# Moving type casts from GpSimd to VectorE and ScalarE, with a new first-load queue and a new order, in a fused attention and SoLU kernel on one Trainium2 core

## The chip, the core and the metric

The kernel runs on one core of a Trainium2 chip. A core has five engines with an instruction queue each: TensorE (PE in the profile, with its weight loads shown apart as PEld), VectorE (DVE), ScalarE (ACT), GpSimd (POOL) and SyncE (SP), which here only issues transfers. All share an on-chip memory (SBUF); matmul results go to a smaller one (PSUM). The engines run side by side and wait for one another through semaphores; each works through its own queue strictly in order. The metric is device time in microseconds (us). The kernel before takes 179.88 us, the median of three runs (179.87 to 180.01).

## What is computed

Batch 4, 8 heads, 768 positions, head dimension 64, 8 global keys, a local window of 96, followed by a 512 to 1024 to 512 feed-forward stage with a SoLU activation and a layer norm:

```python
scores = scale * q @ k.T + bias            # bias: -slope[h] * distance (capped for global keys)
keep   = key is global or 0 <= i - j < 96
a      = softmax(where(keep, scores, -1e9))
x      = (a @ v), heads side by side       # 3072 tokens x 512
h      = x @ w_in                          # 512 -> 1024
solu   = h * softmax(h)
out    = ((solu - mean) / sqrt(var + 1e-6) * g_ln) @ w_out   # 1024 -> 512
```

## The kernel before

The 3072 tokens are cut into twelve **units** of 256 query positions, three for each batch (units 0, 3, 6 and 9 open a batch and have no block of keys to their left). A unit goes through these steps, named by short codes; a number after the code is the unit, a second one a half, a pair of heads or a block of 128 tokens.

- `q`, `k`, `v`: loads of 256 KB each, two for each tensor of a unit, as 32-bit numbers into a ring of 13 staging tiles. The letter in the step is the queue: `S` SyncE, `A` ScalarE, `P` GpSimd.
- `cq`, `ck`, `cv`: the cast of a staged tile of 128 x 1024 from 32 to 16 bits (letter: `D` VectorE, `A` ScalarE, `P` GpSimd). It also frees the staging tile. Lines 138, 140 and 142 are the three engines' casts, in the helper `cast`.
- `tq`, `tk`: eight transposes on TensorE (line 300); `eq`, `ek`: their copy from PSUM (lines 138 and 140 too).
- `S` scores (line 323), `X` exponential (ScalarE, line 332), `M` multiplication by the mask (VectorE, line 339); `gS`, `gX` the same for the global keys, whose keys `gk` (line 314) picks on GpSimd.
- `L` row sums by a matmul with ones (line 385) and with the heads' selector `hm` for the global keys (line 393), `I` their inverse (ScalarE, lines 401 and 402), `V` values, `N` normalisation (VectorE, line 430). `gv0` and `gv` prepare the global values.
- Feed-forward for each 128 tokens: `A` first matmul (line 446), `E` exponential (ScalarE, line 460), `U` product (VectorE, line 468), `Q` squares (ScalarE, line 477), `Z` five tiny operations on GpSimd for the layer norm (lines 492 to 499), `d` a transpose by DMA on SyncE's queue, `O` second matmul (line 522), `o` scaling from PSUM (lines 534 and 536), `st` store.
- Once: `mask` the 16 mask slices on ScalarE from the distances `dist` (VectorE) that come from GpSimd's `off`; `wi` and `wo` the weights' loads; `sc`, `mean`, `ce`, `cm`, `pr`, `sm` fold `g_ln` and the centring into `w_out`. `warm` is a run of matmuls on zeros.

Nothing is planned at run time. A string, `ORDER`, lists all 670 steps, and each engine's queue holds its own steps in the order of that string. What stands ahead of a step on its engine must be done first, whether the step needs it or not. Buffers limit it too: three large PSUM tiles for scores, sums, values and the first feed-forward matmul together, two small ones, and the 13 staging tiles.

In the string before, GpSimd does 23 of the 36 casts, VectorE 10 and ScalarE 3. The opening loads are spread over three queues: `k:P:2:0` and `k:P:2:1` on GpSimd's, `k:A:0:0`, `k:A:0:1`, `k:A:1:1` and `v:A:0:1` on ScalarE's, the rest on SyncE's.

Of the kernel before, what the change touches and what calls it, by code (L numbers as in the profile page):

```python
# [32 lines left out]
q:S:3:1 wi:0 ck:D:5 v:S:1:0 v:S:1:1 ck:P:4 k:P:6:0 k:S:6:1 v:S:2:0 wo:S:6 S:1:3 X:0:1 M:0:1 X:0:2
M:0:2 X:1:0 gX:1 mask:1:4 gv:0 S:1:1 k:S:8:0 X:1:1 mask:1:5 tq:2 M:0:0 X:1:3 eq:D:2 tk:3 M:1:3
ek:D:3 S:1:2 X:1:2 S:2:1 X:2:1 M:2:1 S:2:0 X:2:0 gS:2 gX:2 S:2:2 X:2:2 cq:P:4 M:1:2 M:1:1 M:1:0
S:2:3 X:2:3 M:2:0 M:2:2 tk:4 ek:A:4 cq:P:3 gk:1 wi:2 v:P:2:1 v:S:3:0 wo:S:0 ck:P:6 v:P:3:1 L:0 I:0
tq:4 eq:D:4 L:1 I:1 cq:D:5 tq:3 eq:D:3 k:S:8:1 wo:S:2 q:P:6:0 q:S:6:1 wo:S:4 warm:5:3 V:0 M:2:3
N:0 cv:D:1 S:3:0 X:3:0 S:3:2 X:3:2 tk:5 ek:D:5 gS:4 gX:4 S:3:1 X:3:1 S:4:1 X:4:1 V:1 N:1 M:3:2
q:S:7:0 q:S:7:1 v:S:4:0 v:S:4:1 M:4:1 k:S:7:0 S:3:3 X:3:3 M:3:3 S:4:0 gS:3 X:4:0 tk:6 ek:D:6 S:4:3
X:4:3 gX:3 M:4:0 S:4:2 X:4:2 M:4:3 A:0:0 E:0:0 cv:A:2 A:1:0 E:1:0 A:1:1 M:3:1 U:0:0 M:4:2 Q:0:0  # L40
Z:P:0:0 v:S:5:0 k:S:9:0 tq:5 q:S:8:0 d:S:0:0 cv:P:3 gv0:1 L:2 U:1:0 eq:D:5 E:1:1 U:1:1 M:3:0
d:S:1:0 I:2 sc:D:0 ck:P:8 k:S:10:0 d:S:1:1 A:0:1 E:0:1 v:P:6:0 U:0:1 sc:P:3 sc:A:7 sc:A:6 pr:7
sc:P:2 gS:5 V:2 N:2 gX:5 L:3 I:3 cq:D:6 sc:D:1 gv:1 L:4 I:4 S:5:0 tk:8 ek:D:8 sc:P:4 sc:A:5 A:2:0
E:2:0 U:2:0 X:5:0 tq:6 S:5:1 eq:A:6 X:5:1 mean ce:0 cm ce:1 ce:2 ce:3 ce:4 k:P:7:1 A:2:1 E:2:1
U:2:1 Q:1:1 warm:12 S:5:3 X:5:3 ck:D:7 V:3 cq:P:7 v:P:6:1 S:5:2 pr:6 cv:P:4 N:3 V:4 N:4 k:P:9:1
q:P:8:1 pr:5 sm:5 gk:2 sm:6 Q:2:1 X:5:2 cv:A:6 sm:7 k:P:10:1 M:5:0 tk:7 ek:D:7 S:6:0 S:6:2 X:6:0
M:5:3 Z:P:1:1 gv0:2 Q:0:1 X:6:2 Q:1:0 tq:7 eq:D:7 Z:P:1:0 A:4:0 E:4:0 U:4:0 A:3:0 E:3:0 U:3:0
S:7:2 gS:6 gX:6 O:0:0 o:D:0:0 M:5:2 X:7:2 M:7:2 Q:2:0 v:P:7:0 cq:P:8 q:S:10:0 q:S:10:1 v:S:5:1
q:S:9:0 d:S:0:1 O:1:0 o:D:1:0 Q:3:0 M:5:1 Z:P:3:0 S:6:3 S:6:1 X:6:3 X:6:1 M:6:1 cv:D:5 S:7:0 X:7:0
d:S:3:0 ck:P:9 O:1:1 gS:7 S:7:1 X:7:1 M:7:1 M:7:0 ck:P:10 v:P:7:1 Z:P:0:1 k:S:11:0 k:P:11:1  # L50
q:S:11:0 ck:P:11 d:S:2:0 v:S:9:0 v:S:8:0 cq:D:10 o:A:1:1 S:7:3 X:7:3 cv:P:7 Z:P:2:0 L:5 I:5 A:3:1
M:6:0 E:3:1 M:7:3 gX:7 M:6:2 Q:4:0 Z:P:4:0 U:3:1 A:4:1 O:0:1 E:4:1 tk:9 ek:A:9 o:D:0:1 st:S:0
U:4:1 M:6:3 V:5 N:5 v:S:9:1 q:S:9:1 tq:8 eq:A:8 tk:10 ek:D:10 L:7 I:7 S:8:1 X:8:1 gv:2 A:5:1 E:5:1
st:S:1 v:S:11:0 U:5:1 L:6 I:6 Q:5:1 O:2:0 o:D:2:0 V:6 S:8:3 X:8:3 N:6 gk:3 v:P:11:1 v:P:8:1 S:8:2
Q:3:1 Z:P:3:1 O:3:0 o:A:3:0 X:8:2 M:8:3 cq:D:9 tq:10 A:6:1 E:6:1 eq:D:10 gS:8 gX:8 U:6:1 d:S:2:1
V:7 N:7 S:8:0 X:8:0 Q:4:1 d:S:3:1 tk:11 ek:D:11 M:8:2 M:8:1 d:S:4:0 q:S:11:1 cv:P:9 gv0:3 cq:P:11
Z:P:2:1 tq:9 eq:A:9 A:5:0 E:5:0 U:5:0 A:6:0 E:6:0 U:6:0 gS:10 S:10:0 X:10:0 O:3:1 o:D:3:1 gX:10
Q:5:0 S:10:3 X:10:3 S:9:2 X:9:2 d:S:4:1 d:S:6:0 d:S:5:0 A:7:0 E:7:0 U:7:0 tq:11 eq:D:11 S:10:2
X:10:2 S:10:1 X:10:1 O:2:1 o:D:2:1 M:10:1 Q:6:0 M:8:0 st:S:2 v:S:10:0 st:S:3 A:7:1 Z:P:4:1 cv:P:11
cv:P:8 O:4:0 o:D:4:0 Q:7:0 Q:6:1 E:7:1 d:S:5:1 d:S:6:1 L:8 I:8 S:11:2 X:11:2 M:10:3 U:7:1 M:10:2  # L60
d:S:7:1 gS:11 gX:11 Z:P:6:1 O:4:1 M:10:0 o:D:4:1 M:11:2 Z:P:7:0 v:P:10:1 V:8 N:8 S:11:1 Z:P:5:1
X:11:1 S:11:3 X:11:3 gv:3 O:6:0 S:11:0 X:11:0 S:9:3 X:9:3 Z:P:6:0 L:10 I:10 M:9:3 M:11:1 o:D:6:0
S:9:1 X:9:1 M:9:1 M:11:0 M:9:2 cv:A:10 d:S:7:0 st:S:4 Z:P:5:0 O:5:0 A:8:0 E:8:0 U:8:0 d:S:8:0
o:A:5:0 A:8:1 M:11:3 E:8:1 U:8:1 V:10 gS:9 gX:9 O:6:1 N:10 L:11 I:11 S:9:0 X:9:0 M:9:0 A:10:0
E:10:0 O:5:1 o:A:5:1 o:D:6:1 U:10:0 V:11 L:9 I:9 V:9 N:11 A:11:0:0 A:11:0:1 st:S:6 st:S:5 Q:7:1
Q:8:1 N:9 E:11:0:0 U:11:0:0 d:S:8:1 O:7:0 A:11:1:0 A:11:1:1 o:D:7:0 Q:8:0 Z:P:7:1 Q:11:0:0
E:11:0:1 Z:P:8:0 U:11:0:1 A:9:0 O:7:1 o:D:7:1 st:S:7 Q:10:0 E:11:1:0 U:11:1:0 E:9:0 E:11:1:1
U:11:1:1 O:8:0 t:11:0:0 t:11:0:1 e:D:11:0:0 e:A:11:0:1 o:A:8:0 Z:P:8:1 A:10:1 E:10:1 Q:11:0:1
Z:P:11:0:1 U:9:0 d:S:9:0 d:S:10:0 O:8:1 Q:9:0 Z:P:9:0 Q:11:1:0 Z:P:10:0 O:11:0:0 O:11:0:1
o:A:11:0:0 U:10:1 o:A:11:0:1 Q:10:1 o:D:8:1 st:A:11:0:1 A:9:1 t:11:1:0 t:11:1:1 O:9:0 e:D:11:1:0  # L70
st:S:8 e:D:11:1:1 E:9:1 U:9:1 d:S:10:1 d:S:9:1 O:10:0 O:11:1:0 O:11:1:1 Q:11:1:1 o:A:9:0 O:10:1
Z:P:11:1:1 o:D:11:1:1 st:S:11:1:1 o:D:11:1:0 st:S:11:1:0 st:S:11:0:0 Q:9:1 o:A:10:0 Z:P:10:1
o:A:10:1 st:S:10 O:9:1 Z:P:9:1 o:A:9:1 st:S:9 warm:4:4 warm:5:2 warm:4:5 warm:5:1
"""


# [587 lines left out]
```

## Time and profile before

| what | value |
|---|---|
| time, median of three | 179.88 us |
| profiled span | 178.8 us |
| TensorE busy | 157.3 us, 88% |
| ScalarE busy | 143.8 us, 80% |
| VectorE busy | 125.0 us, 70% |
| GpSimd busy | 107.9 us, 60% |
| DMA | 34.35 MB, mean 192 GB/s |

The shares are averages over stages with different limits, so they are to be read together with the row of 40 slices, which shows the busy tenths of each engine along the span (one slice is 4.47 us). Matmuls are pipelined and their ends modelled, so a TensorE that is shown busy may still be waiting a little between matmuls. The longest waits of the whole trace, summed by line, begin like this (waiting engine and line, what it waited for, us in total, times, longest):

```profile
POOL w L497 <- ACT sq L477: 21.7, 6, 14.1
DVE un L468 <- ACT e L460: 12.7, 11, 2.8
PEld L300 <- POOL q L142: 12.6, 4, 7.4
PE qturned L300 <- POOL q L142: 11.4, 2, 7.4
```

The first is GpSimd idling in the layer norm's small operations; the last two are TensorE waiting for GpSimd's cast of `q`, 7.4 us of it before the very first transpose.

### The profile page before, as it was taken

Reading aid. Unit: us, or ns where it says so; the run is one execution under the profiler, and the core shown is the slowest. Engines: PE = TensorE matmul, PEld = TensorE weight load, DVE = VectorE, ACT = ScalarE, POOL = GpSimd, SP = SyncE. Lnnn points to the kernel's source line nnn. Section 1 sums busy time; section 2 is a strip of 40 time slices with the busy share of each in tenths; the row PEclk is TensorE's granted clock in tenths of the full one; section 3 lists DMA queues with packets and bytes.
Section 4 is the critical chain, followed back from the end, with each engine's and each line's share of the span. In section 5 each row is a group of like instructions: output and inputs, shape, how many; then the busy total and the mean of one; then the engine's idle time right before and its main releaser. Section 6 shows DMA issues by size and latency. Waiting matters only on the chain. (4 is left out here: it accounts for less than half of the span.)

```text
span 178.8 us, 4095 instructions
## 1 busy us (share of the span) xinstructions
PE 157.3 (88%) x1551; PEld 86.0 (48%) x1551; DVE 125.0 (70%) x185; ACT 143.8 (80%) x231; POOL 107.9 (60%) x214
## 2 busy tenths in 40 slices
PE   0227689889995899999999999999999999999987
PEld 0115267564562347445475564545545564544432
DVE  3660999999999579899894878389468364473310
ACT  2474999899999568999979998998893969778720
POOL 8347985721699658779847878708780006407870
PEclk9999957999999699999999999999999999999999
DMA  4999999999999972069999870339991583147553
GB/s 124 341 347 341 339 287 279 356 283 307 235 213 232 274 226 56 6 117 226 156 238 298 187 139 0 59 60 141 292 135 29 176 286 70 49 114 219 114 188 142
DMA packets 50547, 34.35 MB, mean 192 GB/s; under 512 B 41120, under 2 KB 41632, under 8 KB 50528
## 3 DMA queue, kind: packets, MB, share of 16 engines
q1 hardware_dynamic: 45648, 26.35, 61.9%
q0 software_dynamic: 2224, 6.56, 13.6%
q10 hardware_dynamic: 2656, 1.18, 2.4%
q8 instruction: 12, 0.20, 0.5%
q14 instruction: 7, 0.06, 0.1%
HBM read 23.07 MB, written 6.29 MB: 164 GB/s over the span
## 5 line engine op out<-in xcount | busy, mean ns | idle before, releaser
L446 PE MATMUL ph<-w_in,xT 128*128 128x512 f16 x192 | 44.3, 379 | 0.2
L522 PE MATMUL po<-gw,uT 128*128 128x512 f16 x192 | 44.3, 379 | 0.1
L332 ACT ACTIVATE pt<-sc 128x896 f16<-128x896 f32 (+1 forms) x48 | 39.7, 866 | 3.4 <-PE sc L323 3.2
L468 DVE SCALAR_TENSOR_TENSOR un<-e,ph 128x1024 f16<-128x1024 f16 (+1 forms) x26 | 29.4, 1134 | 14.4 <-ACT e L460 12.7
L339 DVE TENSOR_TENSOR pt<-pt,mask 128x896 f16<-128x896 f16 (+1 forms) x48 | 30.0, 659 | 7.9 <-ACT pt L332 7.9
L446 PEld LDWEIGHTS <-xT 128*128 128x128 f16 x192 | 18.2, 98 | 21.5 <-issue 1.0
L522 PEld LDWEIGHTS <-uT 128*128 128x128 f16 x192 | 18.0, 98 | 21.4 <-DMA uT<-un 0.4
L460 ACT ACTIVATE e<-ph 128x1024 f16<-128x1024 f32 (+1 forms) x26 | 24.7, 953 | 2.5 <-DVE un L468 1.2
L477 ACT ACTIVATE sq<-un 128x1024 f16<-128x1024 f16 (+1 forms) x26 | 25.8, 992 | 0.5 <-DVE un L468 0.2
L300 PE MATMUL qturned<-ident,q 128*128 128x128 f16 x96 | 8.6, 242 | 14.6 <-POOL q L142 11.4
L497 POOL TENSOR_SCALAR w<-s,w 128x1 f32<-128x1 f32 x22 | 7.3, 331 | 23.4 <-ACT sq L477 21.7
L323 PE MATMUL sc<-qT,kT 64*128 64x128 f16 (+2 forms) x256 | 15.7, 244 | 1.2 <-DVE xT L430 0.8
L401 ACT ACTIVATE rlb<-lb 128x1024 f32<-128x1024 f32 x12 | 12.3, 1027 | 5.0 <-PE lb L393 5.0
L430 DVE TENSOR_TENSOR xT<-pa,rlb 128x1024 f16<-128x1024 f32 x12 | 14.5, 1218 | 2.1 <-ACT rlb L402 1.7
L499 POOL TENSOR_TENSOR rs<-w,neghalf 128x1 f32<-128x1 f32 x24 | 14.0, 582 | 2.0
L300 PEld LDWEIGHTS <-q 128*128 128x128 f16 x96 | 6.8, 108 | 16.7 <-POOL q L142 12.4
L140 DVE COPY kT<-kturned 128x1024 f16<-128x1024 f16 x9 | 10.8, 1214 | 5.6 <-PE kturned L300 5.6
L534 DVE TENSOR_SCALAR osb<-po,rs 128x512 f32<-128x512 f32 (+1 forms) x15 | 10.6, 712 | 5.4 <-POOL rs L499 2.7
L492 POOL TENSOR_SCALAR w<-s 128x1 f32<-128x1 f32 x22 | 8.6, 393 | 9.1 <-ACT e L460 7.1
L402 ACT ACTIVATE rlb<-rlb 128x1024 f32<-128x1024 f32 x12 | 12.7, 1057 | 0.4
L142 POOL CAST k<-k 128x1024 f16<-128x1024 f32 x8 | 9.2, 1154 | 6.0 <-PE kturned L300 4.9
L495 POOL TENSOR_SCALAR w<-mean,w 128x1 f32<-128x1 f32 x24 | 11.0, 458 | 2.4
(87 smaller groups left out, 243.8 us busy)
## 6 DMA issues: line engine op xcount, KB each, us to landing
...
```

What stands on the lines that cost most here:

```text
L300: nc.tensor.transpose(out=t[:, r], in_=src[:, r].rearrange("p m d -> p (m d)"), identity=held["ident"])
L323: nc.tensor.matmul(out=sc[:, m, o : o + e - a], lhsT=held["kT", u - s + j // 2][r, g, ts(j % 2, P)], rhs=qT[r, g, a:e], start=True, stop=True,
L332: nc.scalar.activation(out=pt[:, :, 0:w], in_=held.pop(("sc", u, g))[:, :, 0:w], func=AF.Exp, scale=inv_sqrt_d)
L339: nc.vector.tensor_tensor(out=pt[:, :, 0:w], in0=pt[:, :, 0:w], in1=held["mask"][:, g, :, o : o + w], op=ALU.mult)
L402: nc.scalar.activation(out=rlb, in_=rlb, func=AF.Exp, scale=-1.0)
L430: nc.vector.tensor_tensor(out=xT.rearrange("p g (r i) -> p g r i", r=2), in0=held.pop(("pa", u)).rearrange("p g (i r) -> p g r i", r=2), i ...
L446: nc.tensor.matmul(out=held["ph", t][:, ts(fh, 512)], lhsT=held["xT", t[0]][:, j, ts(t[1], P)], rhs=held["w_in"][:, j, ts(fh, 512)], start ...
L460: nc.scalar.activation(out=held["e", t][:, f], in_=held["ph", t][:, f], func=AF.Exp, accum_out=s0)
L468: nc.vector.scalar_tensor_tensor(out=held["un", t][:, f], in0=held["e", t][:, f], scalar=1.0, in1=held["ph", t][:, f], op0=ALU.mult, op1=A ...
L477: nc.scalar.activation(out=sq[:, f], in_=held["un", t][:, f], func=AF.Square, accum_out=s2)
L499: eng.tensor_tensor(out=rs, in0=w3, in1=held["neghalf"], op=ALU.pow)
L522: nc.tensor.matmul(out=held["po", t], lhsT=held["uT", t][:, c, :], rhs=held["gw"][:, c, :], start=(c == 0), stop=(c == NFC - 1),)
```

## The change

Four things are done at once.

1. From the fourth unit on, the casts go to VectorE and ScalarE. GpSimd keeps the first three units' (`ck`, `cq` of 0 and 1, `ck` of 2, `cv` of 0, 1 and 2): 8 casts for 23. VectorE has 24 for 10, ScalarE 4 for 3.
2. The first units' loads leave GpSimd's queue and ScalarE's. All `q`, `k` and `v` of units 0 and 1 are issued by SyncE, in the order of need. GpSimd's queue issues 20 loads in all for 23.
3. In `L` the global keys' sums come first and open the accumulation; the local blocks follow.
4. The whole order is new: the two `off` and `dist` steps open GpSimd's and VectorE's queues, unit 0's two transposes are first on TensorE, unit 4's scores come ahead of unit 3's, and so on to the end. The copies `eq`/`ek` stay 17 on VectorE and 7 on ScalarE, though of other units.

The aim is to relieve GpSimd and let the first units begin sooner. The mask's tile is now allocated in `mask`, since a mask is no longer preceded by `cap`. The diff, with the order cut to its beginning:

```diff
 ORDER = """
-zero g:A id gb k:P:2:0 cap off:1 dist:1 fill k:P:2:1 off:0 dist:0 k:A:0:0 k:A:0:1 ck:D:0 q:S:0:0
-q:S:0:1 cq:P:0 tq:0 eq:D:0 hm q:S:1:0 k:S:3:0 q:S:1:1 q:S:2:0 k:S:1:0 k:S:3:1 v:S:0:0 q:S:2:1
-k:S:5:0 mask:1:7 k:A:1:1 mask:0:7 mask:0:0 mask:0:4 selV v:A:0:1 tk:0 cq:P:1 mask:0:1 mask:1:2
-mask:1:1 tq:1 mask:0:2 mask:0:5 ek:A:0 S:0:0 S:0:3 mask:0:6 ck:D:2 tk:2 ek:D:2 k:P:5:1 ck:P:1 tk:1
-ek:D:1 ck:P:3 S:0:1 gk:0 gS:0 eq:A:1 mask:1:3 gS:1 X:0:3 M:0:3 mask:0:3 mask:1:6 mask:1:0 S:0:2
...
+q:S:0:0 k:S:1:0 k:S:0:0 off:1 off:0 zero dist:1 mask:1:0 mask:1:4 id cap dist:0 mask:0:2 mask:0:1
+mask:0:5 mask:0:4 k:S:0:1 ck:P:0 tk:0 ek:D:0 q:S:0:1 cq:P:0 tq:0 k:S:1:1 ck:P:1 q:S:1:0 gb tk:1
+ek:D:1 q:S:1:1 q:S:2:0 q:S:2:1 cq:D:2 mask:1:5 mask:0:0 mask:1:1 mask:0:6 mask:1:6 mask:1:3 eq:A:0
+mask:0:3 S:0:0 gk:0 S:0:2 gS:0 X:0:0 X:0:2 S:0:3 k:S:3:0 S:0:1 X:0:1 cq:P:1 gX:0 fill hm X:0:3
+k:S:2:0 k:S:2:1 ck:P:2 mask:1:7 mask:1:2 mask:0:7 tq:1 eq:D:1 tq:2 S:1:2 X:1:2 S:1:0 X:1:0 eq:D:2
+M:0:3 gS:1 M:0:0 gX:1 S:1:1 X:1:1 v:S:0:0 S:1:3 tk:2 ek:A:2 q:S:4:0 q:S:4:1 cq:D:4 v:S:0:1 M:1:0
+selV X:1:3 k:S:3:1 ck:D:3 wi:0 M:0:1 S:2:1 X:2:1 S:2:3 X:2:3 cv:P:0 S:2:0 gS:2 gX:2 gv0:0 X:2:0
+M:0:2 M:1:2 S:2:2 k:S:4:0 k:S:4:1 tq:4 eq:A:4 M:1:3 tk:3 ek:D:3 gk:1 ck:A:4 X:2:2 L:0 I:0 M:1:1
+gv:0 k:P:6:0 tk:4 q:S:3:0 q:S:3:1 ek:D:4 cq:D:3 L:1 I:1 warm:5:3 M:2:3 tq:3 eq:D:3 v:S:1:0 v:S:1:1
+V:0 N:0 S:4:2 X:4:2 gS:3 S:4:1 X:4:1 M:2:0 wi:2 cv:P:1 k:P:6:1 k:S:5:0 k:S:5:1 ck:D:5 M:4:1 g:S
+k:P:8:0 k:S:8:1 S:3:3 gX:3 X:3:3 S:3:0 X:3:0 v:S:2:0 v:A:2:1 v:S:3:0 V:1 N:1 S:3:2 X:3:2 tk:5
...
 """
...
-        held["mask"] = const.tile([P, NPAIR, 2, W0 + W1], FP16, name="mask")
...
+        if "mask" not in held:
+            held["mask"] = const.tile([P, NPAIR, 2, W0 + W1], FP16, name="mask")
...
-        for g in range(NPAIR):
-            pt = held["pt", u, g]
-            for x, (j, a, e, o) in enumerate(blocks(s)[0]):
-                for m in range(2):
-                    nc.tensor.matmul(
-                        out=lb[m * D : m * D + D, g, a:e], lhsT=held["ones"],
-                        rhs=pt[:, m, o : o + e - a],
-                        start=(x == 0 and g % 2 == 0), stop=True, skip_group_check=True,
-                        tile_position=(0, m * D),
-                    )
         for g in (0, 2, 1, 3):
             rows = slice(64 * (g // 2), 64 * (g // 2) + 64)
             nc.tensor.matmul(
                 out=lb[:, g, i0:UQ],
                 lhsT=held["hm"][rows, 2 * g : 2 * g + 2].rearrange("p h d -> p (h d)"),
-                rhs=held["pg", u][rows], start=False, stop=True, skip_group_check=True,
+                rhs=held["pg", u][rows], start=(g % 2 == 0), stop=True, skip_group_check=True,
             )
+        for g in range(NPAIR):
+            pt = held["pt", u, g]
+            for j, a, e, o in blocks(s)[0]:
+                for m in range(2):
+                    nc.tensor.matmul(
+                        out=lb[m * D : m * D + D, g, a:e], lhsT=held["ones"],
+                        rhs=pt[:, m, o : o + e - a], start=False, stop=True,
+                        skip_group_check=True, tile_position=(0, m * D),
+                    )
```

More of the change, by code (lines that the diff above doesn't have):

```diff
@@ L26 @@
 ORDER = """
-zero g:A id gb k:P:2:0 cap off:1 dist:1 fill k:P:2:1 off:0 dist:0 k:A:0:0 k:A:0:1 ck:D:0 q:S:0:0
-q:S:0:1 cq:P:0 tq:0 eq:D:0 hm q:S:1:0 k:S:3:0 q:S:1:1 q:S:2:0 k:S:1:0 k:S:3:1 v:S:0:0 q:S:2:1
-k:S:5:0 mask:1:7 k:A:1:1 mask:0:7 mask:0:0 mask:0:4 selV v:A:0:1 tk:0 cq:P:1 mask:0:1 mask:1:2
-mask:1:1 tq:1 mask:0:2 mask:0:5 ek:A:0 S:0:0 S:0:3 mask:0:6 ck:D:2 tk:2 ek:D:2 k:P:5:1 ck:P:1 tk:1
-ek:D:1 ck:P:3 S:0:1 gk:0 gS:0 eq:A:1 mask:1:3 gS:1 X:0:3 M:0:3 mask:0:3 mask:1:6 mask:1:0 S:0:2
-k:S:4:0 q:S:4:0 q:S:4:1 k:S:4:1 S:1:0 cv:P:0 gv0:0 cq:P:2 gX:0 q:S:5:0 q:P:5:1 X:0:0 q:P:3:0
@@ L33 @@
[L33 to L73, printed above, removed]
+q:S:0:0 k:S:1:0 k:S:0:0 off:1 off:0 zero dist:1 mask:1:0 mask:1:4 id cap dist:0 mask:0:2 mask:0:1
@@ new lines @@
+M:0:2 M:1:2 S:2:2 k:S:4:0 k:S:4:1 tq:4 eq:A:4 M:1:3 tk:3 ek:D:3 gk:1 ck:A:4 X:2:2 L:0 I:0 M:1:1
+gv:0 k:P:6:0 tk:4 q:S:3:0 q:S:3:1 ek:D:4 cq:D:3 L:1 I:1 warm:5:3 M:2:3 tq:3 eq:D:3 v:S:1:0 v:S:1:1
+V:0 N:0 S:4:2 X:4:2 gS:3 S:4:1 X:4:1 M:2:0 wi:2 cv:P:1 k:P:6:1 k:S:5:0 k:S:5:1 ck:D:5 M:4:1 g:S
+k:P:8:0 k:S:8:1 S:3:3 gX:3 X:3:3 S:3:0 X:3:0 v:S:2:0 v:A:2:1 v:S:3:0 V:1 N:1 S:3:2 X:3:2 tk:5
+M:4:2 M:3:2 M:2:1 S:3:1 X:3:1 M:3:3 q:S:5:0 ek:D:5 q:S:5:1 v:S:3:1 v:S:4:0 gS:4 gX:4 wo:S:6 ck:D:8
+wo:A:0 S:4:0 X:4:0 M:2:2 ck:A:6 S:4:3 X:4:3 M:4:3 M:3:1 wo:S:4 A:0:0 E:0:0 U:0:0 A:1:0 E:1:0 U:1:0
@@ new lines @@
+M:3:0 tk:8 ek:A:8 k:P:7:0 q:P:6:0 q:P:6:1 A:1:1 E:1:1 U:1:1 L:2 I:2 cq:D:6 wo:S:2 M:4:0 v:S:4:1
+A:0:1 E:0:1 L:3 I:3 U:0:1 Q:1:1 cv:P:2 V:2 N:2 cq:D:5 cv:D:3 sc:P:0 tk:6 ek:D:6 k:P:9:0 q:P:7:0
+q:S:7:1 L:4 I:4 A:2:0 E:2:0 tq:5 eq:D:5 sc:D:1 gv0:1 A:2:1 gv:1 U:2:0 sc:A:6 sc:A:7 pr:6 sc:D:4
+E:2:1 U:2:1 Q:0:0 S:5:0 sc:A:5 X:5:0 q:S:8:0 q:S:8:1 warm:12 Z:P:0:0 tq:6 eq:D:6 sc:A:2 Q:1:0 V:3
+N:3 cv:D:4 S:5:3 X:5:3 S:5:1 X:5:1 gS:5 gX:5 sc:P:3 mean cm cq:D:7 S:6:3 X:6:3 ce:0 ce:1 ce:2
+d:S:0:0 V:4 N:4 ce:3 ce:4 pr:7 k:P:7:1 S:5:2 Q:0:1 ck:D:7 v:P:7:0 tq:7 eq:A:7 X:5:2 pr:5 sm:5 sm:6
@@ new lines @@
+sm:7 d:S:1:0 v:S:5:0 v:S:6:0 v:S:6:1 A:3:0 E:3:0 Z:P:1:1 U:3:0 A:4:0 E:4:0 U:4:0 Q:2:1 O:0:0
+o:A:0:0 tk:7 ek:D:7 S:6:2 X:6:2 S:6:1 X:6:1 M:5:3 cq:D:8 M:5:0 gk:2 Z:P:0:1 S:6:0 Z:P:1:0 X:6:0
+O:1:0 M:5:2 cv:D:6 M:5:1 Q:3:0 M:6:2 S:7:2 S:7:0 gS:7 gX:7 o:A:1:0 A:3:1 d:S:1:1 X:7:0 X:7:2 M:7:2
+v:S:5:1 k:S:9:1 Q:4:0 ck:D:9 d:S:0:1 M:6:0 cv:D:5 O:1:1 o:A:1:1 E:3:1 d:S:2:0 k:S:10:0 U:3:1 M:6:3
+q:S:10:0 q:S:11:0 O:0:1 o:A:0:1 gS:6 gX:6 S:7:1 X:7:1 L:5 I:5 q:P:9:0 gv0:2 gv:2 tq:8 M:6:1 eq:D:8
+q:P:9:1 d:S:3:0 V:5 N:5 S:7:3 M:7:1 tk:9 ek:D:9 X:7:3 Q:2:0 Q:3:1 Z:P:2:1 Z:P:2:0 q:S:10:1 v:P:9:0
@@ new lines @@
+k:S:10:1 v:S:9:1 st:S:0 A:4:1 E:4:1 M:7:0 U:4:1 M:7:3 A:5:1 E:5:1 U:5:1 L:6 I:6 gS:8 Z:P:3:1 O:2:0
+gX:8 V:6 N:6 cq:D:10 Q:4:1 Q:5:1 S:8:0 X:8:0 Z:P:4:0 v:P:10:0 Z:P:3:0 L:7 I:7 q:S:11:1 k:S:11:0
+k:S:11:1 gk:3 v:S:7:1 cv:D:7 M:8:0 d:S:3:1 o:D:2:0 cq:D:9 O:3:0 o:D:3:0 v:P:8:0 v:P:10:1 d:S:2:1
+A:6:0 v:S:11:0 V:7 E:6:0 S:8:2 X:8:2 U:6:0 Q:6:0 tq:10 eq:A:10 O:3:1 v:P:8:1 N:7 ck:D:11 S:8:3
+X:8:3 o:D:3:1 S:8:1 ck:D:10 M:8:3 A:7:0 tq:9 eq:D:9 cq:A:11 E:7:0 X:8:1 U:7:0 A:5:0 E:5:0 M:8:2
+tk:10 ek:A:10 A:6:1 tk:11 Q:7:0 U:5:0 Z:P:4:1 ek:D:11 M:8:1 E:6:1 U:6:1 O:2:1 o:D:2:1 d:S:4:0
@@ new lines @@
+Q:5:0 S:10:3 X:10:3 d:S:4:1 st:S:1 S:10:2 X:10:2 M:10:2 cv:D:9 Z:P:5:1 O:4:0 o:D:4:0 cv:D:8 st:S:2
+gS:10 d:S:6:0 S:10:0 X:10:0 gX:10 S:10:1 X:10:1 Q:6:1 L:8 A:7:1 st:S:3 Z:P:7:0 tq:11 eq:D:11
+d:S:6:1 Z:P:6:0 E:7:1 U:7:1 I:8 O:4:1 o:D:4:1 v:P:11:1 M:10:3 st:S:4 d:S:5:1 d:S:5:0 gS:11 V:8 N:8
+d:S:7:0 cv:A:10 S:9:2 S:9:0 X:9:0 M:9:0 cv:D:11 X:9:2 O:6:0 gX:11 Z:P:5:0 Z:P:6:1 S:11:1 X:11:1
+M:10:0 M:11:1 M:10:1 S:11:3 S:11:2 X:11:2 gv0:3 X:11:3 o:D:6:0 M:11:2 O:6:1 o:D:6:1 M:11:3 Q:7:1
+A:8:0 E:8:0 U:8:0 st:S:6 S:11:0 d:S:7:1 L:10 I:10 O:5:0 o:A:5:0 A:8:1 gv:3 X:11:0 M:11:0 E:8:1
@@ new lines @@
+U:8:1 Q:8:1 O:5:1 o:D:5:1 O:7:0 o:D:7:0 gS:9 S:9:1 X:9:1 S:9:3 X:9:3 M:9:3 M:9:1 M:9:2 L:11 I:11
+V:11 N:11 O:7:1 V:10 N:10 gX:9 L:9 I:9 Z:P:7:1 o:D:7:1 V:9 N:9 d:S:8:0 d:S:8:1 A:11:0:0 E:11:0:0
+U:11:0:0 A:11:0:1 E:11:0:1 Q:8:0 Z:P:8:0 A:11:1:0 A:11:1:1 A:10:0 Q:11:0:0 E:11:1:0 E:10:0
+E:11:1:1 U:11:0:1 U:11:1:0 st:S:5 U:10:0 A:9:0 E:9:0 U:9:0 U:11:1:1 O:8:0 o:A:8:0 Q:10:0 O:8:1
+Z:P:8:1 o:D:8:1 t:11:0:0 e:D:11:0:0 A:10:1 t:11:0:1 e:D:11:0:1 st:S:7 d:S:10:0 Z:P:10:0 O:11:0:0
+Q:11:0:1 Q:9:0 E:10:1 U:10:1 Q:11:1:0 Z:P:11:0:1 O:11:0:1 o:D:11:0:0 o:A:11:0:1 Q:11:1:1
@@ L74 @@
+Z:P:11:1:1 A:9:1 t:11:1:0 e:D:11:1:0 t:11:1:1 e:D:11:1:1 st:A:11:0:1 E:9:1 O:10:0 o:A:10:0
+O:11:1:0 U:9:1 O:11:1:1 o:D:11:1:0 st:S:8 Q:10:1 o:A:11:1:1 d:S:9:0 O:9:0 Q:9:1 st:A:11:1:1
+Z:P:9:0 st:S:11:0:0 st:A:11:1:0 Z:P:10:1 d:S:10:1 o:A:9:0 O:10:1 o:D:10:1 d:S:9:1 O:9:1 Z:P:9:1
+o:A:9:1 st:S:10 warm:5:2 warm:4:4 st:S:9 warm:4:5 warm:5:1
 """
```

## The prediction

> **What bounds the kernel now.** I read the page's row of 40 slices first, then sums over chosen stretches, then the timeline of the opening, then the cost of a cast beside a busy neighbour. The page:
>
> ```profile
> PE 157.3 (88%) x1551; PEld 86.0 (48%) x1551; DVE 125.0 (70%) x185; ACT 143.8 (80%) x231; POOL 107.9 (60%) x214
> PE   0227689889995899999999999999999999999987
> DVE  3660999999999579899894878389468364473310
> ACT  2474999899999568999979998998893969778720
> POOL 8347985721699658779847878708780006407870
> PEclk9999957999999699999999999999999999999999
> DMA  4999999999999972069999870339991583147553
> ```
>
> TensorE is nearly empty in the first three slices (13 us), has holes up to slice 13 (58 us) and is full from there to the tail. ScalarE and VectorE are full from slice 5 to 13. The busy time of each engine in three stretches (us from the start, length, then busy time per engine) says the same in numbers:
>
> ```profile
> 5.00:22.00 17.00, 8.00 (x83) 5.50 (x83) 9.70 (x16) 11.43 (x22) 10.28 (x15) 1.00 1.07 343
> 40.00:60.00 20.00, 17.27 (x200) 9.96 (x200) 20.00 (x26) 19.49 (x30) 14.02 (x20) 0.99 1.10 251
> 70.00:150.00 80.00, 79.86 (x825) 42.84 (x824) 58.73 (x85) 71.75 (x111) 48.99 (x96) 1.00 0.72 146
> ```
>
> (The columns are TensorE, its weight loads, VectorE, ScalarE, GpSimd, granted clock, DMA share, GB/s.) So there are three stages. From 5 to 22 nobody is full but the DMA, at 343 GB/s: the opening is bound by data and the hops behind it. From 22 to 60 VectorE (20.00 of 20) and ScalarE (19.49 of 20) are both full. From 70 to 150 TensorE has no idle time; VectorE is at 73% and GpSimd at 61%. **A relief of GpSimd alone buys nothing after 60; an earlier opening is worth its whole length, since what follows is full engines.**
>
> The opening in the timeline:
>
> ```profile
> 14.72 1.03 PE L300 MATMUL qturned<-ident,q 128*128 128x128 f16 x8 [4.00 <-POOL q L142]
> 15.68 0.77 PE L323 MATMUL sc<-qT,kT 64*128 64x224 f16 x8
> 17.17 0.75 ACT L332 ACTIVATE pt<-sc 128x704 f16<-128x704 f32 x1
> 42.60 1.02 ACT L460 ACTIVATE e<-ph 128x1024 f16<-128x1024 f32 x1 [0.19 <-PE ph L446]
> ```
>
> Unit 0's first scores need nothing of unit 1, but `tq:1` stands ahead of them and waits 4.00 us for GpSimd's cast, which stands behind `hm` and `selV`. The first exponential runs at 17.17, the first feed-forward one at 42.60.
>
> And a cast beside a busy neighbour:
>
> ```profile
> 53.24 2.26 DVE L140 CAST q<-q 128x1024 f16<-128x1024 f32 x1
> 53.47 1.35 POOL L568 TENSOR_SCALAR gw<-w_out,g 128x512 f16<-128x512 f32 x2
> ...
> 101.34 0.69 DVE L140 CAST q<-q 128x1024 f16<-128x1024 f32 x1
> 103.84 1.03 POOL L142 CAST v<-v 128x1024 f16<-128x1024 f32 x1
> ```
>
> The same VectorE cast takes 0.69 us alone and 2.26 beside GpSimd.
>
> [...] The pair of 2.26 and 1.35 us above agrees, and so does a tiny GpSimd operation of line 492 that took 1.19 us at 100.88, across a mask product and that cast, for 0.26 elsewhere. [...] the trace has 629 to 694 ns when undisturbed. [...] here eight transposes take 1.03 us up to 28 us into the span and 0.62 after, and the clock row falls at 22 to 29 and near 60. [...] SyncE issues a 256 KB load in about 0.65 us here, the DMA moves it in 262144 B / 343 GB/s = 0.76 us, so one queue keeps pace.
>
> **The change part by part.**
>
> *First loads and opening order.* Unit 0's `k` is whole with the fourth 256 KB load (1.05 MB). Before moves 0.76 MB in the first 5 us and 0.34 MB in each us after, so it lands at 5.8. Cast on GpSimd 1.05 gives 6.9, transposes 1.03 give 7.9, copy on VectorE 1.21 gives 9.1. `q` is the fifth load (6.6), cast 6.9 to 7.9, transposed by 9.0. Its copy is ScalarE's, behind 12 masks. Two 256 KB loads (0.78 and 0.57 us of GpSimd) leave the front of `off`, and `dist:1` opens VectorE, so masks begin near 2.6 for 4.93 before; but ten of the twelve need only that or `dist:0` (done near 5), at 0.42 each (seven took 2.96), so they end near 9.2. Copy 1.02, scores, one mask: first exponential at **11, for 17.17**.
>
> *Is the six us kept?* From there ScalarE is the limit. Its work up to the first feed-forward exponential, by row means: 8 exponentials at 0.753 (6.0), 12 at 0.922 (11.1), five `gX` (2.0), two `I` at 2.08 (4.2), two copies and the two casts `ck:A:4`, `ck:A:6` at about 1.03 (4.1), 3 masks (1.3), two load issues near 0.5 (1.0): 29.7. That gives 11 + 29.7 = 40.7 for 42.60, **1.9 us** earlier. The two casts here are not all extra: ScalarE's remaining copies, casts and foldings after this point fall from 9.9 us (seven at 1.03, three at 0.71, a half copy) to 9.0 (six and four), **0.9** more. VectorE has 8 copies (9.7), 6 casts (4.1), 18 mask products (10.3), two `N` (2.4) and 2.6 of small work, 29.1 us from about 8, so it is ready at 37 and can lose 3 us to GpSimd. Loads: unit 4's `k` is the 20th, at 5.8 + 16 x 0.76 = 18, or 21 with a load of `w_in` between, well ahead of its use near 25. Start: **-2.8 us**.
>
> *Casts, units 3 to 11.* GpSimd loses 15 x 1.05 = 16 us of work; it hides under TensorE, except where TensorE waited for it, which is in the opening. VectorE gains 14 x 0.69 = 9.7 us undisturbed, 14 x 1.1 = 15.4 at the disturbed mean, at most 14 x 2.26 = 32. I take 0.69, since the neighbour that disturbs is largely what leaves: with two thirds of GpSimd's casts gone, mask products that took 1.0 to 1.45 us instead of 0.61 should shorten, some 4 us in all. About eleven of them fall at 60 to 130, 7.6 us on 70, taking VectorE from some 75% to 86% there. Behind each stand a `U` or an `N` that TensorE waits for two matmul groups later; I put **+0.5 us** of new TensorE waits on it, between 0 and 4.
>
> *Global sums first.* The 28 matmuls (20 for a unit that opens a batch) are the same; the wait for `gX` moves ahead of the local ones, and `gX` is earlier in ScalarE's queue than the unit's last `X`. **0**, hidden by TensorE's queue.
>
> *The tail.* Eight-matmul `O` groups end the work in both, with `Z` (2.1 us each, in a row) and the 4.0 us store behind. After the last `A` 7.7 us of TensorE work precede `O:9:1`, against E 1.2 + U 1.3 + transpose 3.9 = 6.4 of hops, so TensorE stays the limit. **0**, within 1.
>
> Sum: -2.8 + 0.5 = -2.3; 179.88 - 2.3 = 177.6. A quieter GpSimd should also spare the stretch at 55 to 60, where TensorE waited 2.4 us for `gv` behind a 2.34 and a 2.26 us operation on VectorE and then ran 3.4 us at half clock. Half of that wait, with the clock left as it is, is 1.0. Forecast **176.6**.
>
> **Rivals.** *VectorE becomes the bound (slower).* It is already full from 22 to 60. If its casts stay at 1.1 us or more, the 14 add 15.4; if 5 us of that reach TensorE over the start's 2.8, the time is 179.88 + 2.2 = **182.1**. For it: 20.00 of 20, and GpSimd still has the `Z` work that collides. Against: disturbed casts cluster where GpSimd casts.
> *The whole opening is kept.* If ScalarE's 5 us idle of 5 to 22 and the clock loss at 22 to 29 and 60 (half of 7 + 3.4, 5.2, partly hidden) go, about 6 us: **174.0**. For it: TensorE works densely from 7 us on. Against: ScalarE's sum.
> *Nothing reaches the end.* The single SyncE queue stalls: before, one load stood there for 9.0 us with a full staging ring and held all behind it. If that eats the lead: **179.9**.
>
> **How the numbers follow.** Forecast 0.57, whole opening 0.15, nothing 0.08, VectorE 0.20. Faster by over 0.2%: the first two less a little, plus part of the third: 0.70. Within: 0.06. Slower: 0.24. The range reaches from half a us under the second case to near the slower one, and leaves a tenth out on each side: 173.5 to 181.3.
>
> **What would show it.** First exponential near 11; first feed-forward exponential near 40.7; VectorE's casts mostly under 0.8 us; VectorE at 86% from 60 to 130 with TensorE still without idle. The prediction is wrong if the first exponential comes after 14, if line 140's casts average over 1.1 us, or if TensorE shows waits for line 468 or 430 in the middle.

## The result, and the profile after

The changed kernel takes 174.86 us (174.73 to 174.96, four runs) against 179.94 (179.87 to 180.29) beside it: a ratio of 0.9713, 95% interval 0.9696 to 0.973, or 5.1 us less. The forecast was 176.6. Medians and ratios here and below are of undisturbed runs alone; some runs of the experiments were slower throughout and are left out, and only the trace of the six loads moved back is of such a run. The page of the changed kernel, without the rows of GpSimd and the DMA:

```profile
PE 154.9 (89%) x1551; PEld 86.1 (50%) x1551; DVE 127.3 (73%) x200; ACT 144.5 (83%) x232; POOL 91.4 (53%) x195
PE   0179599899999989997999999999999958998997
DVE  5079978999899989929989899869837672475310
ACT  5959999899999997769999899999895566796540
PEclk9999759999999999999999999999999999999999
```

A slice is now 4.33 us. TensorE's filling moves ahead by about a slice, and its clock row has lost the dip near 60 us. But there are two new marks in its row: a 7 near 80 us and the pair 5, 8 near 140. GpSimd gave up 16.5 us of work (107.9 to 91.4); VectorE gained only 2.3 (125.0 to 127.3), although it has 14 casts more: its casts took 8.0 us more, its mask products 1.9 less (30.7 to 28.8) and its other work 3.8 less. The three stretches (length, busy us of TensorE, its weight loads, VectorE, ScalarE, GpSimd, then clock, DMA share, GB/s):

```profile
5.00:22.00 17.00, 10.56 (x118) 7.62 (x118) 11.94 (x22) 14.88 (x28) 10.83 (x16) 0.94 1.08 325
40.00:60.00 20.00, 19.95 (x230) 11.08 (x229) 18.82 (x29) 19.78 (x32) 9.87 (x15) 1.00 1.11 268
70.00:150.00 80.00, 76.31 (x788) 40.99 (x787) 59.05 (x91) 68.20 (x110) 43.12 (x89) 1.00 0.71 164
```

From 40 to 60 TensorE is busy 19.95 us where it was 17.27, and VectorE has left its 20.00 of 20. From 70 to 150 it goes the other way: TensorE falls from 79.86 to 76.31. So the change gains early and gives some back late. The timeline of the opening, the first exponential and the first feed-forward one:

```profile
12.18 1.41 ACT L333 ACTIVATE pt<-sc 128x704 f16<-128x704 f32 x2 [0.18 <-PE sc L324]
...
38.41 0.90 ACT L333 ACTIVATE pt<-sc 128x896 f16<-128x896 f32 x1
39.21 1.01 ACT L460 ACTIVATE e<-ph 128x1024 f16<-128x1024 f32 x1
```

They were at 17.17 and 42.60: 5.0 us of lead at the first mark, 3.4 at the second. To follow the lead further I took the starts of the 384 matmuls of lines 446 and 522, which are all of one size, from both traces. The lead is 4.5 us at the 16th and at the last 4.2 (172.31 and 168.06). In between it is larger, 8.1 at the 128th and 9.8 at the 256th, though the order of other work among them differs, so these two are rough; at the 288th it is 4.7. A last part comes behind TensorE, in the tail. The last scaling of the changed kernel:

```profile
168.53 0.69 ACT L536 ACTIVATE osb<-po,rs 128x512 f32<-128x512 f32 x1 [2.42 <-PE po L522]
```

Before, it began at 174.00, 1.7 us after the start of the last matmul, and waited for GpSimd's statistics; now it is 0.5 us after it and waits for the matmul. So 4.25 us from TensorE's end and 1.2 from the tail make the 5.6 by which the profiled span is shorter (178.8 to 173.2), to some 0.1.

The stretch near 60 us, first the kernel before, then the changed one, where eight matmuls average the folded weights:

```profile
59.54 3.56 PE L574 MATMUL gbar<-gw,meanw 128*128 128x512 f16 x8 [0.22 <-DVE kT L140]
```

```profile
58.09 1.90 PE L574 MATMUL gbar<-gw,meanw 128*128 128x512 f16 x8
```

The same eight take 1.66 us less: the granted clock was 0.50 from 59.54 to 62.96 us before, and is 1.00 from 57 to 61 now; the wait of 2.4 us ahead of them (for `gv` on VectorE) is gone too. That is some 4 us in one place, by these two traces.

The fall of the clock is not in every run of the kernel before. In the experiments' sets it ran 47 times: 22 runs with a mean granted clock of 1.00, of 178.5 us in the median, and 25 with a lower one, of 180.0. Runs with a mean of 0.99, which leaves room for one fall of 3.4 us, are as long (five, 180.1 us in the median) as those with 0.96 to 0.97 (18, 180.0), which leave room for the earlier one at 22 us too; so it seems to be the fall near 60 us that costs the 1.5 us, and the earlier one nothing that shows. This is read from the mean clocks; no trace of a run without the fall was kept. The four runs beside the changed kernel (179.87 to 180.29) are all as long as those with it. Of the 5.1 us, then, some 1.5 are not gained on every run of the kernel before.

VectorE's casts, by tensor (busy us, mean ns):

```profile
L140 DVE CAST q<-q 128x1024 f16<-128x1024 f32 x9 | 7.1, 788 | 0.0
L140 DVE CAST v<-v 128x1024 f16<-128x1024 f32 x8 | 5.9, 734 | 0.0
L140 DVE CAST k<-k 128x1024 f16<-128x1024 f32 x7 | 5.4, 768 | 0.3 <-DMA k<-in_k_dram 0.3
```

In all 18.4 us for 24, 0.77 each. Before, ten took 10.4, or 1.04 each. The last column matters below: VectorE's casts wait only 0.3 us for their loads.

### The profile page after: what moved, and what is told of

Its sections match the earlier page's. It is cut to its first block, busy times and chain, and to the rows that moved or that the text cites. A ratio compares the mean times of both kernels' runs of the same rounds, so it can differ in the third digit from the quotient of the medians.

```text
span 173.2 us, 4093 instructions
## 1 busy us (share of the span) xinstructions
PE 154.9 (89%) x1551; PEld 86.1 (50%) x1551; DVE 127.3 (73%) x200; ACT 144.5 (83%) x232; POOL 91.4 (53%) x195
## 4 chain that ended last, share of the span: by engine, by line
PE 66%; POOL 10%; DVE 5%; DMA 5%; ACT 5%; issue 5%; SPq 4%; POOLq 0%; DVEq 0%; ACTq 0%
PE ph L446 21%; PE po L522 20%; PE lb L393 5%; PE pa L412 4%; PE warm L230 4%; SPq L157 4%; PE sc L324 3%; DMA q<-in_q_dram 3%; PE qturned L301 3%; POOL gw L594 2%; DMA v<-in_v_dram 2%; PE kturned L301 2%; DVE q L140 2%; ACT pt L333 2%; PE pa L422 1%
## 5 line engine op out<-in xcount | busy, mean ns | idle before, releaser
L446 PE MATMUL ph<-w_in,xT 128*128 128x512 f16 x192 | 44.9, 379 | 3.1 <-DVE un L468 2.3
L340 DVE TENSOR_TENSOR pt<-pt,mask 128x896 f16<-128x896 f16 (+1 forms) x48 | 28.3, 614 | 5.5 <-ACT pt L333 5.5
L497 POOL TENSOR_SCALAR w<-s,w 128x1 f32<-128x1 f32 x22 | 6.8, 311 | 32.3 <-ACT sq L477 30.6
L301 PE MATMUL kturned<-ident,k 128*128 128x128 f16 x96 | 8.8, 246 | 8.0 <-POOL k L142 8.0
L495 POOL TENSOR_SCALAR w<-mean,w 128x1 f32<-128x1 f32 x24 | 14.5, 605 | 2.4
L499 POOL TENSOR_TENSOR rs<-w,neghalf 128x1 f32<-128x1 f32 x24 | 14.6, 610 | 2.0
L536 ACT ACTIVATE osb<-po,rs 128x512 f32<-128x512 f32 (+1 forms) x11 | 7.1, 650 | 8.5 <-PE po L522 4.5
L324 PEld LDWEIGHTS <-kT 64*128 64x128 f16 x256 | 9.3, 100 | 8.3 <-issue 4.6
L301 PEld LDWEIGHTS <-k 128*128 128x128 f16 x96 | 7.1, 111 | 10.1 <-POOL k L142 8.2
```

What stands on the lines that cost most here:

```text
L301: nc.tensor.transpose(out=t[:, r], in_=src[:, r].rearrange("p m d -> p (m d)"), identity=held["ident"])
L324: nc.tensor.matmul(out=sc[:, m, o : o + e - a], lhsT=held["kT", u - s + j // 2][r, g, ts(j % 2, P)], rhs=qT[r, g, a:e], start=True, stop=True,
L340: nc.vector.tensor_tensor(out=pt[:, :, 0:w], in0=pt[:, :, 0:w], in1=held["mask"][:, g, :, o : o + w], op=ALU.mult)
L446: nc.tensor.matmul(out=held["ph", t][:, ts(fh, 512)], lhsT=held["xT", t[0]][:, j, ts(t[1], P)], rhs=held["w_in"][:, j, ts(fh, 512)], start ...
L495: eng.tensor_scalar(out=w2, in0=mean, scalar1=mean, scalar2=w1, op0=ALU.mult, op1=ALU.subtract)
L499: eng.tensor_tensor(out=rs, in0=w3, in1=held["neghalf"], op=ALU.pow)
```

## The experiments

Two theories were on record. **Theory 1**: the gain is the earlier opening and a denser order; GpSimd's casts were hidden. **Theory 2**: the gain is GpSimd's relief itself. Each kernel ran beside the kernel before on its chip. They ran in three sets, on three chips; in these the kernel before spread from 177.8 to 180.5 us, mostly by the clock, as told above, so their intervals are wider than the first comparison's.

### Casts back in the new order

```diff
-cq:D:3 cq:D:4 ck:D:3 ck:A:4 ck:A:6 ck:D:8 cv:D:3 cv:D:4 cv:D:6 cq:D:7
+cq:P:3 cq:P:4 ck:P:3 ck:P:4 ck:P:6 ck:P:8 cv:P:3 cv:P:4 cv:A:6 cq:P:7
-cq:D:8 cq:A:11 ck:D:9 ck:D:10 ck:D:11 cv:D:7 cv:D:8 cv:D:9 cv:D:11
+cq:P:8 cq:P:11 ck:P:9 ck:P:10 ck:P:11 cv:P:7 cv:P:8 cv:P:9 cv:P:11
```

> The changed kernel with the casts of units 3 to 11 back on the engines of before (19 letters, 15 of them to GpSimd), order and loads kept. Theory 1 (the gain is the earlier opening and the denser order; GpSimd's casts were hidden): 175.5 to 177, VectorE's remaining casts slower than 0.8 us on average. Theory 2 (the gain is GpSimd's relief): near 179, most of the 5 us lost.

(The edit sends 18 of the 19 to GpSimd and one to ScalarE; 15 is the difference in GpSimd's count between the two kernels. So GpSimd has 26 casts, three more than in the kernel before, since it keeps the eight of the first units.) Measured: 184.43 us (two runs, 183.58 and 185.27), ratio 1.0287 (1.0153 to 1.0421). Neither theory has it: it is not back at 179, it is slower than the kernel before. VectorE's remaining casts average 0.72 us, so Theory 1's sign of disturbance did not come there; but its mask products took 34.5 us in all for 28.8 in the changed kernel, so disturbance by GpSimd is not ruled out as a part. TensorE's row in its timeline has two waits:

```profile
27.48 1.04 PE L300 MATMUL kturned<-ident,k 128*128 128x128 f16 x8 [2.08 <-POOL k L141]
...
102.78 0.93 PE L411 MATMUL pa<-pt,v 128*64 128x224 f16 x22 [2.11 <-POOL v L141]
```

TensorE waits for GpSimd's casts, 4.2 us in these two. Its last feed-forward matmul starts 8.6 us later than in the changed kernel (176.7 for 168.1); the rest lies in smaller waits, most of them for VectorE and ScalarE. And GpSimd, in the same trace, itself stood waiting for loads:

```profile
POOL k L141 <- DMA k<-in_k_dram: 12.1, 2, 8.3
```

The shorter of the two, 3.8 us ahead of its first cast, is in the changed kernel too.

A cast set down in the string for VectorE stands, on GpSimd's queue, between other things: behind it, all of GpSimd's work waits for its load; ahead of it, other work must end first. How much of the loss is these waits, how much disturbance and how much the three casts too many, this run does not separate.

### Casts alone in the old order

```diff
-ck:P:3 cq:P:4 cq:P:3 ck:P:6 cv:P:3 ck:P:8 cq:P:7 cv:P:4 cv:A:6
+ck:D:3 cq:D:4 cq:D:3 ck:A:6 cv:D:3 ck:D:8 cq:D:7 cv:D:4 cv:D:6
-cq:P:8 ck:P:9 ck:P:10 ck:P:11 cv:P:7 cv:P:9 cq:P:11 cv:P:11 cv:P:8
+cq:D:8 ck:D:9 ck:D:10 ck:D:11 cv:D:7 cv:D:9 cq:A:11 cv:D:11 cv:D:8
```

> The kernel before with the casts of units 3 to 11 on the engines of the change (18 of the 19 letters; k of unit 4 stays on GpSimd), order and loads of before. Theory 1: 179.5 to 181, no gain by itself, since VectorE is full from 22 to 60 us there. Theory 2: 176 to 177.

Measured: 189.04 us, ratio 1.0513 (1.0409 to 1.0617). Theory 2 falls: the casts alone do not gain, they cost 9 us. Theory 1 had the sign and far too small a size. By the starts of the 384 matmuls this kernel is level with the one before at the 64th (74.7 us and 75.0), 8.3 us late at the 128th (105.8 and 97.5) and 8.5 at the last. Nearly all of the loss so arises in one place, and VectorE's timeline there shows the mechanism:

```profile
91.67 0.69 DVE L139 CAST k<-k 128x1024 f16<-128x1024 f32 x1 [6.92 <-DMA k<-in_k_dram]
92.28 1.08 DVE L139 CAST q<-q 128x1024 f16<-128x1024 f32 x1
93.28 1.05 DVE L139 CAST v<-v 128x1024 f16<-128x1024 f32 x1
94.25 1.48 DVE L338 TENSOR_TENSOR pt<-pt,mask 128x704 f16<-128x704 f16 x3
95.65 1.21 DVE L467 SCALAR_TENSOR_TENSOR un<-e,ph 128x1024 f16<-128x1024 f16 x1
```

The cast of 0.69 us stood 6.92 us at the head of VectorE's queue, waiting for its load, which GpSimd had issued at 85.86. In the kernel before the same cast (`ck` of unit 11) is GpSimd's, and comes after that load in its queue:

```profile
92.02 1.03 POOL L142 CAST k<-k 128x1024 f16<-128x1024 f32 x1 [2.86 <-PE kturned L300]
```

GpSimd idled 2.86 us there, and TensorE only 0.14 in all from 70 to 150 us. On VectorE mask products and `un` stand behind the cast, and TensorE then waited 3.88 us for that `un`, 5.3 us from 90 to 100 in all. Behind the wait its clock was halved from 96.15 to 102.98 us (0.94 in the mean from 70 to 150); half of these 6.8 us, 3.4, is the estimate of what that cost. **What moves with a cast is not its 0.7 us but its wait.**

### The new opening with the old rest, and the reverse

The string of one kernel up to its first `A:0:0`, then what is left of the other's, in the other's order and on its engines:

```diff
 ... gS:4 gX:4 S:4:0 X:4:0 ... M:3:1 wo:S:4
-A:0:0 E:0:0 U:0:0 A:1:0 E:1:0 U:1:0 M:3:0 tk:8 ek:A:8
+(what is left of the string before, from A:0:0 E:0:0 cv:A:2 A:1:0 on)
```

> The changed kernel's steps up to its first feed-forward matmul (188 steps), then all remaining steps in the order and on the engines of before. Theory 1: 176 to 177, first feed-forward exponential near 39.2 us as in the changed kernel, and 2 to 4 us of the gain kept at the end. Theory 2: 178.5 or more, since the casts after that point are GpSimd's again.

> The kernel before's steps up to its first feed-forward matmul (196 steps), then the remaining steps in the order and on the engines of the change. Theory 1: 178 to 179, the first feed-forward exponential at 42.6 us as before and only the stretch near 60 us (no half clock) gained. Theory 2: 176 to 177.

Measured: new opening 176.77 us, ratio 0.9859 (0.9763 to 0.9955); old opening 182.34, ratio 1.0156 (1.0074 to 1.0238). Theory 1 has the first: some 2.5 us of the 5.1 come with the opening, and its clock is full near 60 us (its eight averaging matmuls take 0.38 us each, as in the changed kernel). It is not the opening without any relief of GpSimd, though: six of the 19 moved casts stand in it. Its first feed-forward exponential was at 42.18, not near 39.2: it waited 3.31 us for TensorE, which itself had waited 2.05 us for a cast of `k` on ScalarE and ran at half clock from 38.3 to 41.7 us (0.92 in the mean from 29 to 40, 0.96 from 40 to 60). So the gain kept at the end did not show at that mark. The old opening with the new rest is slower than before by 2.8 us (0.0156 x 179.92), which no theory had: the new rest is only good behind its own opening. In its trace the clock was halved from 149.8 to 153.2 us (0.93 in the mean from 150 to 172), behind a wait of 2.3 us that the changed kernel has too (below); half of 3.4, 1.7 us, is by estimate most of the 2.8.

### Six first loads on their old queues

```diff
-k:S:0:0 k:S:0:1 k:S:1:1 k:S:2:0 k:S:2:1 v:S:0:1
+k:A:0:0 k:A:0:1 k:A:1:1 k:P:2:0 k:P:2:1 v:A:0:1
```

> The changed kernel with six first loads back on the queues of before, in the new order (k of unit 0 and the second half of k of unit 1 and v of unit 0 on ScalarE, k of unit 2 on GpSimd). If what counts is the order of the loads and one SyncE queue keeps pace with the DMA: 174.9 to 175.4, ScalarE's issues (some 0.5 us each) slowing its masks a little. If the queue itself gave the earlier start: 176 or more and a first exponential after 13 us.

Measured: 183.36 us (three runs, 182.45 to 184.78), ratio 1.0235 (1.0156 to 1.0314). The first expectation failed. The second's signs came, with 15.94 us for the first exponential, but not for its reason: it is not a start that the queue as such gives. The timeline, in order of time, shows why:

```profile
5.37 0.58 ACTq L156 DMA_DIRECT2D k<-in_k_dram  x1
...
11.04 1.04 POOL L141 CAST k<-k 128x1024 f16<-128x1024 f32 x1 [7.91 <-DMA k<-in_k_dram]
```

The second half of unit 0's `k` is issued by ScalarE at 5.37, because its place in the string lies behind masks, and masks wait for VectorE's distances. The cast begins at 11.04, where the changed kernel has it at 6.91. Later two loads of unit 2's `k` are issued by GpSimd at 19.83, behind its set-up, and TensorE waits 5.32 us for that cast. A load on a computing engine's queue is issued when that engine gets there. (In the kernel before the two loads of `k` of unit 0 stand ahead of ScalarE's masks; a queue fitted to its place was not tried here.)

### GpSimd's cast ahead of its set-up, in the kernel before

```diff
-... eq:D:0 hm q:S:1:0 ... mask:0:4 selV v:A:0:1 tk:0 cq:P:1 mask:0:1
+... eq:D:0 q:S:1:0 ... mask:0:4 v:A:0:1 tk:0 cq:P:1 hm selV mask:0:1
```

> The kernel before with two of GpSimd's set-up steps (the head selector and the picker of global values) moved from ahead of unit 1's first cast to behind it. The cast then runs some 2.5 us earlier, at about 11 us, and TensorE's 4.00 us wait ahead of the first scores shrinks to 1.5. If the opening is what bounds: 177.5 to 179. If something else (the load of unit 1, or ScalarE's masks) ends last there: 179.5 to 180.

Measured: 178.46 us, ratio 0.9949 (0.9923 to 0.9975), 21 runs, within the first expectation. Moving two words, and no cast to another engine, gives a fifth of the gain:

```profile
10.72 1.50 POOL L141 CAST q<-q 128x1024 f16<-128x1024 f32 x1 [3.88 <-DMA q<-in_q_dram]
12.28 1.03 PE L299 MATMUL qturned<-ident,q 128*128 128x128 f16 x8 [2.08 <-POOL q L141]
...
14.74 0.75 ACT L331 ACTIVATE pt<-sc 128x704 f16<-128x704 f32 x1
```

The first exponential comes at 14.74 for 17.17 and the first feed-forward one at 40.69 for 42.60. Of those 1.9 us the ratio keeps 0.9 (0.0051 x 179.9). That is likely too little: 19 of the 21 runs have a mean clock under 1.00, and its trace has the fall near 60 us; they are 1.5 us below the runs of the kernel before that have such a clock (178.5 and 180.0). The cast now waits for its load, so the rest of the opening is the DMA's order.

### The row sums

Only the body of `sums` is exchanged, in the changed kernel and in the kernel before.

```diff
-for g in (0, 2, 1, 3):   # global keys, start=(g % 2 == 0)
-for g in range(NPAIR):   # local blocks, start=False
+for g in range(NPAIR):   # local blocks, start=(x == 0 and g % 2 == 0)
+for g in (0, 2, 1, 3):   # global keys, start=False
```

> The changed kernel with only the row sums put back: the local blocks first and opening the accumulation, the global keys last. If the order inside the sums is worth nothing (the same matmuls, and the global exponential is done well ahead): 174.9 within 0.3. If the early global matmuls fill time in which TensorE would wait for the last mask product of a unit: up to 1 us slower.

Measured: 176.37 us, ratio 0.9837 (0.9784 to 0.9891). Since the changed kernel had not run on that chip, both ran again side by side:

> The changed kernel as it is, beside the next three on the same chip, so that the row sums are compared with it directly: ratio to before 0.970 to 0.978.

> The changed kernel with the local row sums first again, now beside the changed kernel. If the inner order is worth nothing: its ratio lies within 0.3% of that of the changed kernel. If it is worth about 1 us, as the ratio 0.9837 against 0.9713 from different calls would have it: 0.5 to 1.2% above.

> The kernel before with only the row sums changed: global keys first. If it is worth nothing: ratio 0.998 to 1.002. If it fills TensorE's waits: 0.99 to 0.996.

Measured: changed kernel 175.35 us, ratio 0.9792 (0.9737 to 0.9846), a little over what was expected; with local sums first 176.39, ratio 0.984 (0.9778 to 0.9902); the kernel before with global sums first 179.63, ratio 0.999 (0.9954 to 1.0027). In the kernel before the order is worth nothing that shows. In the changed one the difference has the same sign as in the first comparison and is 0.5%, 0.9 us, but the intervals overlap. And the times of both lie in two groups: four runs of the changed kernel at 174.8 to 175.5 and two near 176.4; three with local sums first at 175.2 to 175.6 and three at 177.2 to 177.5. The kept traces are of the upper groups, and in that of the changed kernel the clock was 0.50 behind the wait at 141 us that comes next. Its two upper runs have a mean clock of 0.971 and the other four 0.98 to 0.99; with local sums first it is 0.981 for the upper three and 0.98 to 0.99 for the others. So part of the 0.9 may be how often the clock fell. The worth of the order stays open, between 0 and about 1 us.

### The wait at 141 us

TensorE's longest waits in the changed kernel, after the one for its very first cast:

```profile
PE ph L446 <- DVE un L468: 2.3, 1, 2.3
PE sc L324 <- ACT kT L138: 1.8, 1, 1.8
PE gs L353 <- ACT osb L536: 1.3, 1, 1.3
```

The first stands in unit 11: its first matmul's second half follows, in the string, the exponential and product of the first half.

```diff
-A:11:0:0 E:11:0:0 U:11:0:0 A:11:0:1 E:11:0:1
+A:11:0:0 A:11:0:1 E:11:0:0 U:11:0:0 E:11:0:1
```

> The changed kernel with one step moved: the second half of the first feed-forward matmul of unit 11 directly behind its first half, ahead of the exponential and the product of the first half. In the changed kernel it stands behind them and waits 2.34 us for VectorE's product, though it writes the other half of the tile. If that wait is on the path, 172.5 to 173.3; if the time is only lost again in the tail, 174.5 or more.

Measured: 172.85 us, ratio 0.9642 (0.9589 to 0.9695), the lower of the two ranges. TensorE at that place in the changed kernel, then with the move:

```profile
140.02 1.04 PE L446 MATMUL ph<-w_in,xT 128*128 128x512 f16 x4
143.40 0.81 PE L446 MATMUL ph<-w_in,xT 128*128 128x512 f16 x3 [2.34 <-DVE un L468]
```

```profile
140.17 4.06 PE L445 MATMUL ph<-w_in,xT 128*128 128x512 f16 x18
```

Eighteen matmuls, all that the view holds up to its end at 144 us, run without a break where four did. The last of the 384 starts at 166.1 for 168.1: 2.0 of the 2.3 us reach the end. The changed kernel did not run on this chip; its ratios, 0.9713 and 0.9792, are 0.7 and 1.5 points above.

The move spares more than the wait in some runs. In the later trace of the changed kernel (of a run of 176.37 us) the same wait of 2.34 us stands ahead of 143.34, and the clock was then halved (the granted clock here is the 0.50):

```profile
143.00:146.40 3.40, 3.06 (x8) 1.11 (x8) 0.72 (x3) 1.16 (x3) 0.00 (x0) 0.50 0.00 0
```

In the first trace (174.96 us) the clock stayed full there (1.00 from 142.6 to 146.1). None of the six runs with the move is over 174 us, where two of the ten of the changed kernel came to 176.4.

Why the second half waited for the first half's product is not shown. A second move was put on top:

```diff
-... k:S:9:1 Q:4:0 ck:D:9 ... o:A:1:1 E:3:1 d:S:2:0
+... k:S:9:1 ck:D:9 ... o:A:1:1 E:3:1 Q:4:0 d:S:2:0
```

> The same move, and the squares of unit 4's first block moved behind the scaling of unit 1 and the next exponential on ScalarE, so that the small PSUM tile that TensorE waits 1.34 us for at 77.5 us comes free about 1.1 us earlier. If both waits are on the path: 171.5 to 172.5. If only the first: as the kernel with the first move alone.

Measured: 172.80 us, ratio 0.9638 (0.9592 to 0.9685), no different from the first move alone, though the intervals leave room for half a us. The wait of 1.3 us at 77.5 shrinks to 0.31, and TensorE's list has a new one:

```profile
PE pv L369 <- ACT osb L535: 1.0, 1, 1.0
```

By these lines it only changed its place: the next step that needs a small PSUM tile now waits for the same kind of scaling.

## Why the prediction was right, and where its steps were not

**The opening (-2.8 us): right in kind and near in size.** First exponential forecast at 11, measured 12.18; unit 0's `k` was cast at 6.91, where 5.8 was worked out, since the load came later. First feed-forward exponential forecast at 40.7, measured 39.21: ScalarE took 27.0 us between the two marks, not 29.7. Its terms were near right: the times of ScalarE's instructions between the marks add up to 29.7 us in the trace of the changed kernel as well. The sum failed as a length, since each instruction begins about 0.1 us before the one ahead of it is shown to end: 38.41 and 0.90 make 39.31, and the next begins at 39.21. The lead there is 3.4 us. That an earlier opening carries gain is shown by the two words moved (0.9949), with all casts in place, and fits the new opening with the old rest (0.9859).

**The stretch near 60 us (-1.0 us): mis-sized.** Half the wait was taken and the clock left as it was. In fact the whole wait went and the clock stayed full, 2.4 + 1.66 = 4.1 us by the two traces. The second term is partly luck: about half the runs of the kernel before do not have the fall.

**The casts (+0.5 us): the duration was nearly right, the mechanism was missed.** 0.77 us each for 0.69; VectorE is at 82% from 60 to 130 us (57.52 of 70) for the 86% forecast. Mask products shortened by 1.9 us for the 4 forecast. But "it hides under TensorE" failed as a statement on casts. The forecast priced the instructions and not the wait for the load that stands with each in an in-order queue. With the casts back in the new order the kernel lost 9 us on the changed one (ratios 1.0287 and 0.9792 to the kernel before); with the casts alone in the old order it lost 9 on the kernel before (1.0513). Neither is the worth of the casts: both are in the main the price of a letter that does not fit its place. What the casts bring by themselves, with an order made for each case, no run here shows.

**New TensorE waits (0 to 4 us): they came, in a place not named.** The prediction called waits for line 468 or 430 in the middle a sign that it is wrong, and both came: 0.74 us for line 430 at 64 us and 2.34 for line 468 at 141, the latter on the path. By its own mark it was wrong here. It was not VectorE being full, though: one step moved took the longer one away. That is why the time is 174.9 and not near 172.9.

**The tail (0, within 1): 1.2 us.** The last scaling no longer waits for GpSimd's statistics. The prediction saw TensorE as the limit and did not count that GpSimd's five operations ended later still.

**The sums (0):** shown for the kernel before; open, up to about 1 us, for the changed one.

In sum, by TensorE's busy time in the two traces: its idle time in the first 40 us fell from 16.6 to 12.3 us; from 40 to 170 us it grew from 3.0 to 5.1, the wait near 60 us gone and those at 64, 77.5 and 141 us come; the clock near 60 spared 1.7 us and the tail 1.2. That makes 4.3 - 2.1 + 1.7 + 1.2 = 5.1, the measured gain. The forecast of 3.3 us came as near as it did partly by luck: it missed 3.1 us near 60 and 1.2 in the tail on the one side, and some 4 us of new waits, for 0.5, on the other. **The rivals:** VectorE did not become the bound; the SyncE queue did not stall the lead away, and when loads left it the kernel was slower. The case of the whole opening kept, 174.0, came nearest in number. It had counted on the clock near 60, which did come, and on the one at 22 to 29 us, which did not: the changed kernel ran at half clock from 19.8 to 26.7. Of the opening 3.4 of 5.0 us were kept, and the tail it did not have.
